# Two frequency-domain filters with a gate: a padded scratch and another order of its rows

## The chip, the core and the metric

The kernel runs on one core of a Trainium2 chip. A core has five engines with instruction streams of their own: TensorE (PE, with a separate stream of weight loads, PEld), VectorE (DVE), ScalarE (ACT), GpSimd (POOL) and SyncE (SP), which here only issues DMAs. The DMAs of a core are carried out by 16 DMA engines between the device memory (HBM) and the on-chip memory (SBUF, 128 partitions). The metric is the device time of one execution in microseconds.

## The reference

An input `x` of 2048 x 1024 goes through two filters, A and B: a real 2-D Fourier transform, a product with a complex weight (one per filter), and the inverse transform. A gate per row, from a dot product of the row with `gate_w`, mixes the two results.

```python
def _A_ref(x, w_r, w_i):                       # B alike
    X = rfft2(x.astype(float32), axes=(-2, -1))
    W = w_r + 1j * w_i
    X = X * W
    return irfft2(X, s=(S, D), axes=(-2, -1)).astype(bfloat16)

x = A_x
g = sigmoid((x * gate_w).sum(-1, keepdims=True))
out = g * _A_ref(x, A_w_r, A_w_i) + (1 - g) * _B_ref(x, B_w_r, B_w_i)
```

Both filters see the same `x`, so the forward transform is made once.

## The kernel before

All transforms are matrix products with constants. The 1024 columns are split into even and odd frequencies (`par` 0 and 1), and the 2048 rows are transformed in two steps (a transform over 64 and one over 32). The order of all work is written out by hand in the string `ORDER`, one token per step; a letter names the step, the numbers its unit, and the letters behind the colon the engines that move its results out of the accumulator (PSUM). A scheduler adds nothing: each engine runs its instructions in the order in which the tokens issue them.

- `r`, `f`, `E`, `O` (`f1`): first step of the forward transform, from `x` into `Y`.
- `F` and `G` (`f2`, `f3`): the transform along the columns and the second step along the rows, for 16 units `n` of 128 frequencies (`n` from 0 to 7 even, from 8 to 15 odd half).
- `w` (`load_w`, L229): the weights of a unit from HBM, most of them issued ahead of the string; `c` (`cmul`, L416) multiplies by them; `d` (`edge`) does the edge columns.
- `i` (`i1`, L454): first step of the inverse transform of a unit. Its constant is `WI`, made by `make_constants` on the host, whose columns set the order of the 128 rows that come out. When both of its halves are done, the result (`rl`, 128 partitions x 4 blocks x 1 KB) is stored in the scratch in HBM by one DMA on SP's queue (L462).
- `q` (`fetch`, L471): a DMA on SP's queue that reads rows of four units back from the scratch, onto 64 partitions (even or odd ones, by `g`) of 8 KB each. `q1.0.2` reads for the odd half, units 0 to 3 of it, quarter `v` = 2 of the rows. The scratch thus does a transposition: what was spread over partitions within one unit comes to lie along one partition. SP waits for the stores of these four units before it issues the first of their reads.
- `j` (`i2`, L484): second step of the inverse transform, with the gate in its constants (`EAB`). Its `v` runs from 0 to 7, and two of them share one quarter: `j1.0` and `j1.1` need `q1.0.0` and `q1.1.0`; `j1.2` and `j1.3` need `q1.0.1` and `q1.1.1`; `j1.4` and `j1.5` those of quarter 2, `j1.6` and `j1.7` those of quarter 3.
- `k`, `D` (`i3`, `i3d`), `s` (`fold`) and `t` (`last`): the inverse transform along the columns, the sums and differences, and the stores of the output (L568 to L583).

The scratch is one tensor per half, of 8 units x 4 blocks x 128 rows x 1 KB, so a block is 128 KB and a unit 512 KB. Row `p` of a block is partition `p` of `rl`; in the order made by `be` in `make_constants`, the row is (j, v, c, r) with j of 2, v of 4, c of 2 and r of 8, and the eight rows of an r are one piece of 8 KB:

```python
sc = [scratch.tile([NU, 4, P, 512], BF16, name=f"sc{par}") for par in range(2)]
nc.sync.dma_start(sc[par][u].rearrange("t p f -> p t f"), rl[:].rearrange("p t a r m -> p (t a) (r m)"))
src = sc[par][4 * g:4 * g + 4].rearrange("u t (j v c r) f -> (u t j) v c (r f)", j=2, v=4, c=2)
nc.sync.dma_start((XP, RP)[par][v][g::2, 0:4096], src[:, v])
```

A read of quarter `v` takes 64 pieces: from each of 16 blocks the pieces (j, c) of that `v`, in this order on consecutive partitions of the target. `row_of` puts the rows of the gate's constant in the same order.

SP's queue, in order, holds the loads of `x`, constants and weights up to 28 us, then from 30 us the 16 stores and 16 reads of the scratch among the last weight loads, a late constant (`l`, L253) at 76 us, the eight reads of the odd half from 78 us, and the output from 90 us.

Of the kernel before, what the change touches and what calls it, by code (L numbers as in the profile page):

```python
# [10 lines left out]
P = 128  # L11
# [3 lines left out]
NU = 8  # L15
N1 = 32
N2 = 64
BF16 = mybir.dt.bfloat16
# [38 lines left out]
def _bf16np(a):  # L57
    return np.ascontiguousarray(np.asarray(a, dtype=np.float32).astype(ml_dtypes.bfloat16))


def block_k2(b):
    return (0, 32) if b == 0 else (b, 64 - b)


def block_rows(b):
    return np.array([k2 + 64 * k1 for k2 in block_k2(b) for k1 in range(N1)])
# [7 lines left out]
def row_of(ab, t, j, c):  # L74

    return 2 * (16 * (t // 2 % 4) + 8 * (t % 2) + 4 * ab + 2 * j + c) + t // 8


def make_constants():
    c = {}  # L80
    s2 = np.arange(N2)
    F = np.zeros((N2, 32, 2))
    EZ = np.zeros((32, 2, N2))
    E = np.zeros((P, N2))
    for b in range(32):
        k2 = block_k2(b)[0]
        th = 2 * np.pi * s2 * k2 / 64
        if b == 0:
            comps = (np.ones(64), np.cos(np.pi * s2))
            F[:, 0, 0], F[:, 0, 1] = comps  # L90
            EZ[0, 0], EZ[0, 1] = comps
        else:
            comps = (np.cos(th), np.sin(th))
            F[:, b, 0], F[:, b, 1] = np.cos(th), -np.sin(th)
            EZ[b, 0], EZ[b, 1] = 2 * np.cos(th), -2 * np.sin(th)
        for ab in range(2):
            for cc in range(2):
                E[row_of(ab, b // 2, b % 2, cc)] = comps[cc]
    F = F.reshape(N2, 64)
    F1 = np.concatenate([F, -F, F], axis=1)  # L100
    c["F1"] = _bf16np(np.concatenate([F1, F1], axis=0))
    c["E"] = _bf16np(E)
    c["EZ"] = _bf16np(EZ.reshape(64, 64) / 64)
    d = np.arange(256) + 0.5
    i = np.arange(256)
    FD = np.zeros((2, 2, 256, 256))
    IG = np.zeros((2, 2, 256, 256))
    for par in range(2):
        m = 2 * i + par
        ph = 2 * np.pi * np.outer(d, m) / D  # L110
        FD[par, 0] = np.cos(ph)
        IG[par, 0] = 2 * np.cos(ph).T
        if par == 0:
            IG[0, 0, 0] = 1
        m = 2 * i + (2 if par == 0 else 1)
        ph = 2 * np.pi * np.outer(d, m) / D
        FD[par, 1] = -np.sin(ph)
        IG[par, 1] = 2 * np.sin(ph).T
        if par == 0:
            IG[0, 1, 255] /= 2  # L120
    IG /= S * D
    c["FD"] = _bf16np(FD.reshape(2, 2, 2, 128, 256).transpose(3, 0, 2, 1, 4).reshape(128, 2, 1024))
    IGS = np.stack([-IG[1, 1], IG[1, 1]], axis=1).reshape(2, 128, 2, 256)
    c["IGU"] = _bf16np(IGS.transpose(1, 0, 2, 3).reshape(128, 1024))
    c["IG"] = _bf16np(IG.reshape(2, 2, 2, 128, 256).transpose(3, 0, 1, 2, 4).reshape(128, 2048))
    s1 = np.arange(N1)
    WF = np.zeros((P, NT, 3, 64))
    WI = np.zeros((P, NT, 4, 64))
    for t in range(NT):
        for j in range(2):  # L130
            b = 2 * t + j
            k = block_rows(b)
            al = np.zeros((2, N1, 64), dtype=complex)
            for p in range(64):
                w = np.exp(-2j * np.pi * k[p] * s1 / S)
                if b == 0:
                    al[p // 32, :, p] = w
                else:
                    al[0, :, p] = w
                    al[1, :, p] = 1j * (1 if p < 32 else -1) * w  # L140
            be = al.conj()
            if b > 0:
                be[1] = -be[1]
            al = al.transpose(1, 0, 2).reshape(64, 64)
            be = be.reshape(64, 64).T
            be = be.reshape(64, 2, 4, 8).transpose(0, 2, 1, 3).reshape(64, 64)
            h = slice(64 * j, 64 * j + 64)
            WF[h, t, 0], WF[h, t, 1], WF[h, t, 2] = al.real, al.imag, -al.imag
            h = h if t % 2 == 0 else slice(64 - 64 * j, 128 - 64 * j)
            WI[h, t, 0], WI[h, t, 1], WI[h, t, 2], WI[h, t, 3] = be.real, be.imag, -be.imag, -be.real  # L150
    c["WF"] = _bf16np(WF)
    c["WI"] = _bf16np(WI)
    c["SG"] = np.where(np.arange(P) // 8 % 2 == 0, 1.0, -1.0).astype(np.float32).reshape(P, 1)
    return c
# [3 lines left out]
def gated_mix(ctx, tc, x_in, we_in, wo_in, first_in, out):  # L158
    nc = tc.nc
    cn = make_constants()  # L160
    dr = {n: nc.inline_tensor(a, name=f"cst_{n.lower()}").ap() for n, a in cn.items() if n not in ("F1", "SG")}
    w_in = (we_in, wo_in)
# [15 lines left out]
    def take(tag, *dims):  # L178

        t = slots[tag][int(next(order[tag]))][:, 0:int(np.prod(dims))]  # L180
        ax = "abcd"[:len(dims)]
        return t.rearrange(f"p ({' '.join(ax)}) -> p {' '.join(ax)}", **dict(zip(ax, dims)))

    def halves():
        return [bank(), bank()]
# [24 lines left out]
    Ec = const.tile([P, N2], BF16, name="ec")  # L210
    Ez = const.tile([64, N2], BF16, name="ez")
    scratch = ctx.enter_context(tc.tile_pool(name="scratch", bufs=1, space=bass.MemoryType.DRAM))
    sc = [scratch.tile([NU, 4, P, 512], BF16, name=f"sc{par}") for par in range(2)]
    Y = big.tile([P, 2, 2, 2, 16, 2, 32, 2], BF16, name="y")
    y = [Y[:, par] for par in range(2)]
    wod = [big.tile([P, 2048], BF16, name=f"wo{k}") for k in range(4)]
# [45 lines left out]
    def evac(eng, out, in_):  # L262
        if eng == "A":
            nc.scalar.copy(out=out, in_=in_)  # L264
        else:
            nc.vector.tensor_copy(out=out, in_=in_)  # L266
# [6 lines left out]
    def hp(j):  # L273
        return slice(64 * j, 64 * j + 64)
# [168 lines left out]
    def i1(n, r, eng="A"):  # L443
        par, u = n // NU, n % NU
        p = Ps[n]
        o = 1 if par == 0 and r == 1 else 0
        ps = halves()
        terms = (((0, 0, 0), (2, 0, 1), (3, 1, 1), (2, 1, 0)), ((1, 0, 0), (0, 0, 1), (2, 1, 1), (0, 1, 0)))[r]
        terms = [z for z in terms if z[1:] not in summed.get(n, ())]
        for k, (w, q, a) in enumerate(terms):  # L450
            for tt in range(2):
                for j in range(2):
                    hin = hp(j ^ tt)
                    nc.tensor.matmul(ps[tt][hp(j), :], lhsT=WI[hin, 2 * u + tt, w, :],  # L454
                                     rhs=p[hin, q, tt, a::2, o:o + 256], start=(k == 0), stop=(k == len(terms) - 1))
        if r == 0:
            RLs[n] = take("rl", 2, 2, 2, 256)
        rl = RLs[n]
        for tt in range(2):
            evac(eng[tt % len(eng)], rl[:, tt, :, r, :], ps[tt][:].rearrange("p (a m) -> p a m", a=2))  # L460
        if r == 1:
            nc.sync.dma_start(sc[par][u].rearrange("t p f -> p t f"), rl[:].rearrange("p t a r m -> p (t a) (r m)"))  # L462
            RLs.pop(n), Ps.pop(n)

    def rows(par, v):
# [1 line left out]

    def fetch(par, g, v):

        src = sc[par][4 * g:4 * g + 4].rearrange("u t (j v c r) f -> (u t j) v c (r f)", j=2, v=4, c=2)  # L470
        nc.sync.dma_start((XP, RP)[par][v][g::2, 0:4096], src[:, v])  # L471

    Vs, EVs = {}, {}
# [114 lines left out]
    def run(tok):  # L588
        op, a, e = tok[0], tok[1:].split(":")[0], tok.split(":")[1] if ":" in tok else ""
        n = [int(q) for q in a.split(".")] if a else []  # L590
        if op in "rfEO":
            f1(((n[0], 0), (n[0], 1)) if op in "rf" else ((n[0], "EO".index(op)), (n[0] + 1, "EO".index(op))), e)
        elif op in "VQ":
            xfold(n[0], op)
        elif op == "y":
            gate_weights()
        elif op == "h":
            gt["z"] = gate_hat()
        elif op == "l":
            late()  # L600
        else:
            dict(F=f2, G=f3, d=edge, c=cmul, i=i1, w=load_w, g=gate_z, q=fetch, j=i2, k=i3, D=i3d,
                 s=fold, a=part, t=last)[op](*n, *([e] if e else []))
# [61 lines left out]
```

## Time and profile before

| What | Value |
|---|---|
| Median of 3 runs | 108.09 us (108.0 to 108.25) |
| The profiled execution | 107.94 us |
| Its span, first to last instruction | 106.2 us |
| Mean granted TensorE clock | 0.995 |
| DMA: bytes moved, mean rate | 37.06 MB, 349 GB/s |
| HBM read / written | 24.23 MB / 12.58 MB |
| Packets under 8 KB / all | 15840 / 16881 |
| SP's queue: share of 16 DMA engines | 92.4% |
| Stores and reads of the scratch together, issue to landing | 3.7, 5.9, 8.5 us (least, median, most) |
| Reads alone | 4.2, 6.5, 8.2 us |

The profile is of one execution. Busy times are the sums of an engine's instructions; the rest of the span is idle time. A row such as "PE pt L484 <- DMA ro<-sc: 1.5, 2, 1.2" in the list of waits says who waited (engine, tile, line), for whom, and how long in total, how often and at most. `pt` are accumulator tiles, `xr` and `ro` the SBUF tiles that hold first `x` and weights and later the rows read from the scratch (`xr` for the even, `ro` for the odd half). The DMA share is the mean busy share of the 16 DMA engines; it can exceed 1 in a short stretch, because a packet is booked whole where it starts. GB/s is what they moved. `SPq` and `PEldq` are the sequencers of SP and of the weight loads.

### The profile page before, as it was taken

How to read it: one execution, taken by the hardware profiler on the slowest of the kernel's cores; microseconds unless marked ns; L12 is line 12 of the kernel's file. 1: busy time of each engine (PE TensorE's matmuls, PEld its weight loads, DVE VectorE, ACT ScalarE, POOL GpSimd, SP SyncE). 2: the span in 40 equal slices, each digit the busy share in tenths (PEclk: the TensorE clock that was granted, in tenths of full speed). 3: DMA queues.
4: the chain of work that ended last, by engine and by line, in shares of the span. 5: the costliest groups of instructions: out<-in, count | busy, mean ns of one | idle time of the engine just before them, and what ended most of it. 6: DMA issues, size and time to landing. Idle time of an engine off the chain costs nothing. (4 is left out here: it accounts for less than half of the span.)

```text
span 106.2 us, 3918 instructions
## 1 busy us (share of the span) xinstructions
PE 97.6 (92%) x1606; PEld 66.3 (62%) x1608; DVE 90.5 (85%) x141; ACT 93.9 (88%) x187; POOL 8.5 (8%) x14
## 2 busy tenths in 40 slices
PE   5989999989999999999999999999999698999740
PEld 2378989655655766555765567667899485754530
DVE  1459998298999997999999999999989959899970
ACT  5069989998999999999999999999999878999740
POOL 1000001018880001000000000000000000000000
PEclk9999999999999999999999999999999999999997
DMA  2999999999999999999999699979989989967994
GB/s 44 336 350 420 402 395 396 406 422 397 398 405 410 399 379 358 394 367 368 374 371 387 204 376 384 367 278 342 358 264 279 355 321 377 409 275 321 392 350 133
DMA packets 16881, 37.06 MB, mean 349 GB/s; under 512 B 1628, under 2 KB 10464, under 8 KB 15840
## 3 DMA queue, kind: packets, MB, share of 16 engines
q1 hardware_dynamic: 16272, 36.37, 92.4%
q10 hardware_dynamic: 560, 0.45, 1.5%
q8 instruction: 12, 0.20, 0.7%
q14 instruction: 5, 0.04, 0.1%
q0 software_dynamic: 32, 0.00, 0.0%
HBM read 24.23 MB, written 12.58 MB: 347 GB/s over the span
## 5 line engine op out<-in xcount | busy, mean ns | idle before, releaser
L454 PE MATMUL pt<-p,wi 64*64 64x512 bf16 x504 | 30.3, 377 | 0.1
L264 ACT CAST rl<-pt 128x512 bf16<-128x512 f32 x47 | 25.6, 707 | 0.1
L416 DVE TENSOR_TENSOR p<-X,ro 128x4096 bf16<-128x4096 bf16 x11 | 25.2, 2294 | 0.0
L264 ACT CAST T<-pt 128x512 bf16<-128x512 f32 (+1 forms) x40 | 21.7, 623 | 0.9 <-PE pt L533 0.5
L454 PEld LDWEIGHTS <-wi 64*64 64x64 bf16 x504 | 15.1, 106 | 10.7 <-issue 0.8
L264 ACT CAST V<-pt 128x512 bf16<-128x512 f32 x29 | 17.2, 743 | 1.3 <-PE pt L484 1.3
L264 ACT CAST X<-pt 128x512 bf16<-128x512 f32 x29 | 16.8, 671 | 0.0
L376 PE MATMUL pt<-fd,y 128*128 128x256 bf16 x128 | 15.9, 273 | 0.0
L264 ACT CAST y<-pt 128x512 bf16<-128x512 f32 x21 | 11.1, 631 | 4.5 <-PE pt L298 3.2
L376 PEld LDWEIGHTS <-y 128*128 128x128 bf16 x128 | 11.6, 98 | 4.2 <-issue 2.9
L266 DVE CAST rl<-pt 128x512 bf16<-128x512 f32 x17 | 11.3, 683 | 0.1
L499 PE MATMUL pt<-ig,V 128*128 128x256 bf16 x88 | 10.8, 273 | 0.0
L395 PE MATMUL pt<-T,wf 64*64 64x512 bf16 (+2 forms) x192 | 9.4, 307 | 0.0
L575 DVE TENSOR_TENSOR rl<-wo,T 128x1024 bf16<-128x1024 bf16 (+1 forms) x16 | 8.9, 620 | 0.6 <-ACT T L264 0.5
L264 ACT CAST p<-pt 128x512 bf16<-128x512 f32 x14 | 9.3, 818 | 0.0
L552 DVE TENSOR_TENSOR wo<-p,pt 128x512 bf16<-128x512 bf16 x14 | 8.8, 682 | 0.6 <-ACT p L264 0.5
L416 DVE TENSOR_TENSOR p<-X,wo 128x4096 bf16<-128x4096 bf16 x4 | 9.1, 2281 | 0.0
L499 PEld LDWEIGHTS <-V 128*128 128x128 bf16 x88 | 8.0, 98 | 1.5 <-issue 0.4
L370 POOL TENSOR_SCALAR ro<-ro 128x8 bf16<-128x8 bf16 x7 | 7.0, 1013 | 23.2 <-DMA ro<-in_we_dram 23.2
L307 PE MATMUL pt<-f,xr 64*128 64x256 bf16 x112 | 7.1, 270 | 0.5 <-DMA xr<-in_x_dram 0.5
L266 DVE CAST y<-pt 128x512 bf16<-128x512 f32 x11 | 7.2, 684 | 0.4 <-PE pt L310 0.4
L281 DVE TENSOR_TENSOR rl<-xr 128x512 bf16<-128x512 bf16 x7 | 3.0, 424 | 4.7 <-DMA xr<-in_x_dram 4.6
(58 smaller groups left out, 98.8 us busy)
## 6 DMA issues: line engine op xcount, KB each, us to landing
sc<-rl SPq DMA_DIRECT2D x16, 512.0 KB, 5.5
xr<-sc SPq DMA_DIRECT2D x8, 512.0 KB, 6.3
ro<-sc SPq DMA_DIRECT2D x8, 512.0 KB, 6.6
ro<-in_we_dram SPq DMA_DIRECT2D x7, 516.0 KB, 8.6
xr<-in_x_dram SPq DMA_DIRECT2D x6, 512.0 KB, 7.4
out_dram<-rl SPq DMA_DIRECT2D x6, 512.0 KB, 3.2
wo<-in_wo_dram SPq DMA_DIRECT2D x4, 512.0 KB, 7.7
ro<-in_wo_dram SPq DMA_DIRECT2D x4, 512.0 KB, 6.5
```

Source lines behind the costliest of these rows:

```text
L264: nc.scalar.copy(out=out, in_=in_)
L266: nc.vector.tensor_copy(out=out, in_=in_)
L281: e.tensor_tensor(f[:, 0, :], x[j][:, 0:512], x[j][:, 512:1024], ALU.add)
L307: nc.tensor.matmul(pv[h][:, :, c, :, :].rearrange("p a e k -> p e a k"), lhsT=xs(j0, h, q), rhs=fs(h, 0, *st), start=(q == 0), stop=(q == 3))
L370: nc.gpsimd.tensor_scalar(Ws[n][:, :, :, 257:258], Ws[n][:, :, :, 256:257], -1.0, None, ALU.mult)
L376: nc.tensor.matmul(ps[tt][:, e * 256:e * 256 + 256], lhsT=y[par][:, c, e, t].rearrange("p b s k -> p (b s k)"), rhs=FD[:, par, c, e, :], s ...
L395: nc.tensor.matmul(ps[tt][ho, dst:dst + ln], lhsT=WF[hp(j), 2 * u + tt, w, :], rhs=T[hp(j), tt, src:src + ln], start=(k == 0), stop=(k == 2))
L416: nc.vector.tensor_tensor(po, xo, wo, ALU.mult)
L454: nc.tensor.matmul(ps[tt][hp(j), :], lhsT=WI[hin, 2 * u + tt, w, :], rhs=p[hin, q, tt, a::2, o:o + 256], start=(k == 0), stop=(k == len(te ...
L499: nc.tensor.matmul(po, lhsT=V[:, s, 2 * r + c, :], rhs=IG[:, par, 2 * r + c, :], start=(c == 0), stop=(c == 1))
L552: (nc.vector if eng == "V" else nc.gpsimd).tensor_tensor(ev[:, :, r, :], c_, s_, op)
L575: nc.vector.tensor_tensor(o4[:, k, h] if not isinstance(od, list) else o4[:, k.start, h], x, y_, op)
```

## The change

Three things, in one:

- Each block of 128 rows in the scratch gets 32 more rows that nothing writes or reads. Blocks lie 160 KB apart instead of 128, a unit takes 640 KB instead of 512.
- `make_constants` no longer reorders the columns of `be`. A unit's rows then come out as (c, v, r) within j. Seen as one index c of 4 (j and the old c), the row of a block is (c, v, r).
- The read takes from each of the 16 blocks four pieces of 8 KB that are 32 KB apart. Before, they were at 0, 8, 64 and 72 KB of a block, plus 16 KB times `v`; after, at 0, 32, 64 and 96 KB, plus 8 KB times `v`. The order of the 64 pieces on the target's partitions is the same, and so are `row_of` and all that follows.

```diff
@@ make_constants
             al = al.transpose(1, 0, 2).reshape(64, 64)
             be = be.reshape(64, 64).T
-            be = be.reshape(64, 2, 4, 8).transpose(0, 2, 1, 3).reshape(64, 64)
             h = slice(64 * j, 64 * j + 64)
@@ gated_mix
-    sc = [scratch.tile([NU, 4, P, 512], BF16, name=f"sc{par}") for par in range(2)]
+    sc = [scratch.tile([NU, 4, P + 32, 512], BF16, name=f"sc{par}") for par in range(2)]
@@ i1
         if r == 1:
-            nc.sync.dma_start(sc[par][u].rearrange("t p f -> p t f"), rl[:].rearrange("p t a r m -> p (t a) (r m)"))
+            nc.sync.dma_start(sc[par][u, :, 0:P].rearrange("t p f -> p t f"), rl[:].rearrange("p t a r m -> p (t a) (r m)"))
@@ fetch
-        src = sc[par][4 * g:4 * g + 4].rearrange("u t (j v c r) f -> (u t j) v c (r f)", j=2, v=4, c=2)
+        src = sc[par][4 * g:4 * g + 4].rearrange("u t p f -> (u t) p f")[:, 0:P].rearrange("k (c v r) f -> k v c (r f)", c=4, v=4)
         nc.sync.dma_start((XP, RP)[par][v][g::2, 0:4096], src[:, v])
```

## The prediction

> **What bounds the kernel now.** I read the page first: the busy times, the slices, and how long a DMA takes to land. A read of the scratch is `ro<-sc` or `xr<-sc`, a store `sc<-rl`.
>
> ```profile
> span 106.2 us, 3918 instructions
> PE 97.6 (92%) x1606; PEld 66.3 (62%) x1608; DVE 90.5 (85%) x141; ACT 93.9 (88%) x187; POOL 8.5 (8%) x14
> ...
> sc<-rl SPq DMA_DIRECT2D x16, 512.0 KB, 5.5
> xr<-sc SPq DMA_DIRECT2D x8, 512.0 KB, 6.3
> ro<-sc SPq DMA_DIRECT2D x8, 512.0 KB, 6.6
> ```
>
> Three engines stand between 85 and 92% over the whole span, so a DMA matters only where they run dry. The list of waits names those places for the scratch:
>
> ```profile
> PE pt L484 <- DMA ro<-sc: 1.5, 2, 1.2
> ...
> PEld L484 <- DMA ro<-sc: 0.6, 1, 0.6
> ```
>
> No row names `xr<-sc`: the eight reads of the even half are in time. Of the odd half two are late, and the timeline says when:
>
> ```profile
> 78.13 7.70 SPq L471 DMA_DIRECT2D ro<-sc  x8
> ...
> 85.05 1.00 PEld L484 LDWEIGHTS <-ro 128*128 128x128 bf16 x32 [1.43 <-issue]
> 85.08 1.09 PE L484 MATMUL pt<-eab,ro 128*128 128x64 bf16 x32 [1.18 <-DMA ro<-sc]
> ...
> 88.48 0.99 PEld L484 LDWEIGHTS <-ro 128*128 128x128 bf16 x32 [0.64 <-DMA ro<-sc]
> 88.48 1.11 PE L484 MATMUL pt<-eab,ro 128*128 128x64 bf16 x32 [0.36 <-DMA ro<-sc]
> ```
>
> TensorE starts `j1.0` at 85.08 after 1.18 us of nothing (it waits for reads 1 and 2 of this half, q1.0.0 and q1.1.0) and `j1.2` at 88.48 after 0.36 us (reads 3 and 4). ScalarE and VectorE drain with it. Here the program is bound by scratch reads; after `j1.2` the three engines are the bound again, since reads 5 and 6 land just as `j1.4` loads its weights (issued at 83.89, landing 7.1 us later: 91.0; weights at 91.09).
>
> Third, how fast these reads run: stretches of 1 us with TensorE, weight load, VectorE, ScalarE, GpSimd, and last the clock, DMA share and GB/s.
>
> ```profile
> 81.00:82.00 1.00, 1.00 (x19) 0.91 (x16) 0.81 (x3) 1.00 (x4) 0.00 (x0) 1.00 0.86 254
> 82.00:83.00 1.00, 1.00 (x12) 0.90 (x10) 1.00 (x2) 1.00 (x4) 0.00 (x0) 1.00 0.78 197
> 83.00:84.00 1.00, 0.89 (x9) 0.56 (x6) 1.00 (x3) 1.00 (x4) 0.00 (x0) 1.00 0.94 385
> 84.00:85.00 1.00, 0.00 (x0) 0.00 (x0) 0.89 (x2) 0.60 (x2) 0.00 (x0) 1.00 1.06 410
> ...
> 87.00:88.00 1.00, 1.00 (x11) 0.76 (x8) 1.00 (x3) 1.00 (x4) 0.00 (x0) 1.00 0.98 352
> ...
> 90.00:91.00 1.00, 0.95 (x5) 0.49 (x5) 1.00 (x2) 1.00 (x4) 0.00 (x0) 1.00 1.03 434
> ```
>
> A read moves 64 pieces of 8 KB. Share x 16 engines, divided by the pieces moved (GB/s / 8.192 per us), is the time of one piece on one DMA engine: 1.03 x 16 / 53 = 0.311 us at 90 to 91, but 0.444 us at 81 to 82 and 0.519 us at 82 to 83, 0.365 us at 87 to 88. Same size, same row, same queue, up to 1.7 times as long. A packet is booked whole where it starts, so one row is rough; sums over several are better. From 81 to 90, where almost nothing but these reads is under way, the shares sum to 8.38 and the pieces to 365: 134.1 us of engine time against 365 x 0.311 = 113.6 us. The excess is 20.5 / 16 = 1.28 us: 0.57 us of it from 81 to 83, 0.11 us from 83 to 85, 0.45 us from 85 to 88, 0.15 us to 90. This excess is the only thing of the kernel that addresses alone can change, and it lies ahead of the two waits.
>
> **The change part by part.** *The constants.* The reordering of the 64 columns of `be` is host work; WI keeps its size, and the 504 matmuls of L454 stay 377 ns each. Nothing. The order of instructions on every engine is the same but for line numbers.
>
> *Bytes and counts.* 16 stores of 512 KB, 16 reads of 64 pieces of 8 KB, as before; the gap is never written or read. The source of a read goes from 32 x 2 pieces to 16 x 4. SP issues a read in 0.60 us (median of the `ro<-sc` issues, 0.51 to 1.52); the nearest other row, a store with eight times the pieces, takes 0.37 us, so I take nothing for the issue, bounded by some 0.2 us either way on the first two reads.
>
> *The stores.* Each partition's four 1 KB pieces go 160 KB apart instead of 128. From 75 to 78 stores are nearly alone: mean share 1.06 at 362 GB/s, or 1.06 x 16 / 353 = 0.048 us a piece; the fastest stretch of them (77 to 78) has 0.047. There is nothing to gain in their rate. But the last store gates read 2: SP waits 1.68 us for it, until 80.4. Were it 0.6 us earlier, the whole 1.18 us could go; this is the far end. I take zero.
>
> *The reads.* Before, the pieces of one read sit at multiples of 64 KB plus 0 and 8 KB: pairs of 16 KB, all at one place within 64 KB. After, they sit at (5k + c) x 32 KB, k the block (0 to 15) and c the piece (0 to 3): if each engine works at one k, the sixteen stand on sixteen different multiples of 32 KB within 512 KB, where before they stood on the same one within 128 KB. The trace shows no such address pattern. Bounds: excess gone altogether (all pieces at 0.311 us, as at 90 to 91 with the old layout): 1.28 to 0 us. Or all pieces as slow as at 81 to 82: 365 x 0.133 / 16 = 3.0 us. The excess is largest where all engines start together after a gap in the reads (81 to 83) and zero once they have been running unevenly for a while, which looks like sixteen streams in step meeting at one place; spreading them bears on just that. Between the two rows (0.311 late, 0.444 to 0.519 early) I take half of the excess away, 0.64 us.
>
> In time: read 2 lands 0.29 us earlier (half of 0.57), so `j1.0` starts at 84.79. Reads 3 and 4 landed at 88.5 (issued at 81.7, 6.8 us); they come half of 1.13 = 0.57 us earlier, at 87.9, and `j1.2` wants them at 88.12 - 0.29 = 87.83. So `j1.2` starts at 87.9, 0.57 us earlier. Reads 5 and 6 land at 91.0 - 0.64 = 90.36; `j1.4` wants them at 91.09 - 0.57 = 90.52. Every later step is engine work that shifts along. **Sum: -0.6 us**, from a span of 106.2 to 105.6. This profiled execution took 107.94 us, 1.74 outside the span; the median of the runs is 108.09, 0.15 above it. Forecast 107.5.
>
> The Trainium skill speaks against it. On its page "DMA: Bandwidth & Descriptors", section "Latency and other measured facts", copies with rows 512 KiB apart still run at 207 GB/s a direction beside 214 for the padded layout, and only pitches of 2 MiB and up lose much (164, then 103). By that rule 128 KB is harmless and the sum is 108.1. The trace agrees in part: the pieces at 90 to 91 have the same pitch and lose nothing; it disagrees in that the pieces at 82 to 83 lose 0.2 us each.
>
> **The rivals.** *Addresses have nothing to do with it.* The excess comes from starting on an idle queue and from reading behind a burst of stores. For it: it fades with time since the last store (80.4), and at 78 to 79, where the late constant in rows of 2 KB shares the engines with the tail of the stores, the rate falls to 182 GB/s with a share of 0.84. Against it: at 85 to 88, 5 us past any store, 0.45 us are still lost. Time: 108.1. The rule of the Trainium skill named above leads to the same time.
>
> *The reads get worse.* Before, two pieces are one run of 16 KB and four reads walk through one run of 64 KB; after, no two pieces of a read touch. If a visited stretch stays quick to read, half of the pieces lose that. For it: the quick pieces at 90 to 91 are the last of a run whose neighbours were read just before. Price: excess up by half, `j1.0` +0.29, read 4 +0.57, so `j1.2` starts 0.57 late: 108.7. Doubled: read 4 +1.13, read 6 +1.28 of which 0.15 more: 109.3. At 3.0 us of excess: 2.37 times 1.13 is 1.55 us late, 109.7. It decides from the first piece lost, since neither wait has slack.
>
> *The read isn't spread as before.* Sixteen outer rows in place of 32 might be dealt to the engines less evenly, or the issue takes longer. Against it: 16 rows suit 16 engines. Some 0.5 us on read 2: 108.6 or more.
>
> **How the numbers follow.** Forecast 0.46; addresses without effect 0.18; reads worse 0.30; spread or issue worse 0.06. About 0.2% (0.2 us) is what a measurement of this kernel tells from no change. Faster 0.46, same 0.18, slower 0.36. The fast end takes the excess away whole (-0.93: `j1.0` 0.57, then the 0.36 of `j1.2`) and the last store 0.6 us sooner: -1.5, 106.6; the slow end is the doubled excess, 109.3. The forecast's own range is 106.9 to 107.8.
>
> **What would show it.** In the profile after: the wait of L484 on `ro<-sc` falls from 1.5 us to about 0.9; GB/s just after the first odd reads start rise from 197 and 254 to 300 or more; `ro<-sc` lands in some 6.1 us instead of 6.6; stores stay at 5.5. The forecast is wrong if those stretches stay at 0.44 us a piece or more, if the loss sits in stores, or if new waits on `xr<-sc` appear before 80 us.

## The result, and the profile after

The change makes the kernel slower: 114.32 us median of 6 runs (112.81 to 115.38) against 108.09 us before, a ratio of 1.0487 with a 95% interval of 1.0426 to 1.0547. Executions of one kernel fall into fast and slow ones, some per cent apart: here and below a median counts all, a ratio only the fast ones, and the traces of nat_pad4, nat_pad16, nat_pad128, same_places_16x4 and whole_odd are of slow ones. The profiled execution took 112.81 us with a span of 111.0 us, 4.8 us more than before. The code is one line shorter, so L483 here is L484 of before (`i2`), L470 is the read of the scratch and L461 the store.

The page of the changed kernel first: busy times, then the DMA issues with their size and the time from issue to landing.

```profile
PE 98.0 (88%) x1608; PEld 65.3 (59%) x1608; DVE 90.7 (82%) x141; ACT 94.4 (85%) x187; POOL 8.5 (8%) x14
...
sc<-rl SPq DMA_DIRECT2D x16, 512.0 KB, 5.6
xr<-sc SPq DMA_DIRECT2D x8, 512.0 KB, 8.7
ro<-sc SPq DMA_DIRECT2D x8, 512.0 KB, 8.5
```

The engines do almost the same work as before (98.0 us against 97.6 on TensorE, 94.4 against 93.9 on ScalarE). The median store lands as fast (5.6 against 5.5 us), reads of the scratch take some 2 us longer (8.7 and 8.5 against 6.3 and 6.6). The list of waits of the changed kernel shows who paid:

```profile
PE pt L483 <- DMA ro<-sc: 4.4, 4, 2.2
...
DVE rl L265 <- DMA sc<-rl: 2.2, 2, 1.7
...
ACT rl L263 <- DMA sc<-rl: 1.2, 2, 0.6
...
PE pt L483 <- DMA xr<-sc: 0.7, 1, 0.7
```

The last three are new. The even half's reads are now late too (`xr<-sc`), and VectorE and ScalarE wait for stores to leave the `rl` buffers. The median hides these stores: the three issued from 61 us land in 7.1 to 7.8 us where they took 5.6 to 6.7, and the last five, issued from 70 us on, in 4.5 to 5.7 where they took 3.7 to 4.6. That they lie behind the slow reads on the same queue is the likely reason; no view shows it directly. The timeline of the changed kernel gives the places:

```profile
65.20 0.64 PE L483 MATMUL pt<-eab,xr 128*128 128x64 bf16 x16 [0.70 <-DMA xr<-sc]
68.31 0.69 DVE L265 CAST rl<-pt 128x512 bf16<-128x512 f32 x1 [1.66 <-DMA sc<-rl]
...
87.81 1.09 PE L483 MATMUL pt<-eab,ro 128*128 128x64 bf16 x32 [2.23 <-DMA ro<-sc]
...
91.71 1.11 PE L483 MATMUL pt<-eab,ro 128*128 128x64 bf16 x32 [0.86 <-DMA ro<-sc]
...
95.85 0.63 PE L483 MATMUL pt<-eab,ro 128*128 128x64 bf16 x16 [1.15 <-DMA ro<-sc]
```

Against the same steps before, the delay grows in this way:

| Step | Before, us | After, us | Later by |
|---|---|---|---|
| `j0.0` starts | 64.32 | 65.20 | 0.9 |
| last store of the scratch issued | 75.8 | 77.7 | 1.9 |
| `j1.0` | 85.08 | 87.81 | 2.7 |
| `j1.2` | 88.48 | 91.71 | 3.2 |
| `j1.4` | 91.31 | 95.85 | 4.5 |
| `j1.6` | 94.84 | 99.71 | 4.9 |
| `j1.7` | 98.76 | 103.63 | 4.9 |

So 1.9 us come from the even half and the stores behind it, 3.0 us from the odd half's reads, and nothing behind them. How fast these reads run is seen in the stretch from 86 to 93 us (columns: TensorE, weight load, VectorE, ScalarE, GpSimd, granted clock, DMA share, GB/s), first before, then after:

```profile
86.00:93.00 7.00, 6.58 (x98) 4.83 (x96) 6.59 (x13) 6.61 (x15) 0.00 (x0) 1.00 0.95 375
```

```profile
86.00:93.00 7.00, 4.33 (x81) 3.50 (x82) 4.67 (x10) 4.11 (x9) 0.00 (x0) 1.00 1.02 262
```

All 16 DMA engines are busy and move only 262 GB/s. By the arithmetic of the prediction (share x 16, divided by pieces of 8 KB per us) one piece keeps an engine 1.02 x 16 / 32.0 = 0.51 us, where it was 0.95 x 16 / 45.8 = 0.33 us. It stays at 262 in nearly every microsecond of this stretch: a ceiling, not a loss at the start.

### The profile page after: what moved, and what is told of

It reads as the page before. It is cut to its first block, busy times and chain, and to the rows that moved or that the text cites. A ratio compares the mean times of both kernels' runs of the same rounds, so it can differ in the third digit from the quotient of the medians.

```text
span 111.0 us, 3920 instructions
## 1 busy us (share of the span) xinstructions
PE 98.0 (88%) x1608; PEld 65.3 (59%) x1608; DVE 90.7 (82%) x141; ACT 94.4 (85%) x187; POOL 8.5 (8%) x14
## 5 line engine op out<-in xcount | busy, mean ns | idle before, releaser
L263 ACT CAST V<-pt 128x512 bf16<-128x512 f32 x29 | 16.0, 644 | 4.0 <-PE pt L483 3.9
L483 PE MATMUL pt<-eab,ro 128*128 128x64 bf16 x128 | 4.7, 193 | 4.4 <-DMA ro<-sc 4.4
L263 ACT CAST p<-pt 128x512 bf16<-128x512 f32 x14 | 8.3, 700 | 0.0
L483 PEld LDWEIGHTS <-ro 128*128 128x128 bf16 x128 | 4.3, 98 | 6.1 <-issue 4.7
```

The source lines that it names most:

```text
L483: nc.tensor.matmul(ps[s][:, ch * 128 + h * 64:ch * 128 + h * 64 + 64], lhsT=R[:, k, ch * 128:ch * 128 + 128], rhs=EAB[:, 4 * v + k, :], st ...
```

## The experiments

Three things changed at once: the order of the rows, the gap, and with them the way in which a read's source is told to the DMA. Each kernel below is the changed one with an edit; "a piece" is the time of one 8 KB piece on one DMA engine, worked out as above from a stretch of the odd half's reads. The fences show the main lines of each edit; the others are left out.

### Order alone, and smaller gaps

```diff
-    sc = [scratch.tile([NU, 4, P + 32, 512], BF16, name=f"sc{par}") for par in range(2)]
+    sc = [scratch.tile([NU, 4, P, 512], BF16, name=f"sc{par}") for par in range(2)]   # nat_pad0; P + 4, P + 8, P + 16 in the others
```

> Natural order alone, blocks 128 KB apart, nothing unused. Theory PLACE (a read is slow when all of its 8 KB pieces stand on the same place within 32 KB): pieces still stand on one place, so as slow as the change: 112 to 115 us, 0.45 to 0.52 us of a DMA engine per 8 KB piece in the odd half's reads. Theory GAP (the 160 KB distance of the blocks does the harm): back to 107.5 to 108.5 us and 0.31 to 0.37 us a piece. Theory RUN (what is lost is that two pieces were one run of 16 KB): 112 to 115 us.

> Natural order, 4 KB unused behind each block: eight places 4 KB apart within 32 KB. PLACE: 106.5 to 108.5 us, 0.31 to 0.36 us a piece. GAP: 108 to 112 us, a small gap harms less. RUN: 112 to 115 us.

> Natural order, 8 KB unused behind each block, so that the blocks of one read stand on four places within 32 KB. PLACE: 106.5 to 108.5 us, 0.31 to 0.36 us a piece. GAP: a gap harms, 110 to 115 us. RUN: still no two pieces touch, 112 to 115 us, 0.45 to 0.52 us a piece.

> Natural order, 16 KB unused behind each block: two places within 32 KB. PLACE: between the others, 107 to 110 us, 0.33 to 0.42 us a piece. GAP: 110 to 115 us. RUN: 112 to 115 us, 0.45 to 0.52 us a piece.

Without a gap the natural order is as fast as the kernel before: 107.86 us median against 107.89, ratio 0.9982 (0.994 to 1.0024). Each gap, of 4, 8 or 16 KB, is as bad as 32: ratios 1.051 (1.0392 to 1.0628), 1.0597 (1.0484 to 1.071) and 1.0515 (1.0388 to 1.0642), with 0.53, 0.55 and 0.57 us a piece (90 to 97 us). That a small gap harms less, 108 to 112 us at 4 KB, was expected under GAP and is not so: the median there is 113.69 us. nat_pad0 from 87 to 91 us, then nat_pad8 from 90 to 97:

```profile
87.00:91.00 4.00, 2.98 (x45) 2.04 (x44) 3.96 (x10) 3.04 (x7) 0.00 (x0) 1.00 1.01 422
```

```profile
90.00:97.00 7.00, 5.67 (x63) 3.64 (x62) 5.65 (x12) 4.88 (x9) 0.00 (x0) 0.82 1.02 241
```

nat_pad0 needs 1.01 x 16 / 51.5 = 0.31 us a piece with no two pieces touching and all of them at one place within 32 KB: RUN and PLACE fall. Of what was written down only GAP is left. But a gap does two things: it moves addresses, and it keeps the source from being joined. Without it, 16 blocks of 4 pieces lie 32 KB apart throughout and are told as 64 pieces at one distance; with it, as 16 x 4. The kernel before was told as 32 x 2. This is read off the code; no view shows the list that reaches the DMA engines.

### The same places told in another way, and gaps told in another way

```diff
# same_places_16x4: no gap; the four pieces of a block from last to first, and the gate's rows with them
-    return 2 * (16 * (t // 2 % 4) + 8 * (t % 2) + 4 * ab + 2 * j + c) + t // 8
+    return 2 * (16 * (t // 2 % 4) + 8 * (t % 2) + 4 * ab + 3 - 2 * j - c) + t // 8
+        t = sc[par][4 * g:4 * g + 4]
+        src = bass.AP(t.tensor, t.offset + 49152 + 4096 * v, [[65536, 16], [-16384, 4], [1, 4096]])
# nat_pad128: P + 128 rows a block
# half_pad16: 16 rows unused behind every 64 (half_pad0: none), a store in two halves, 32 x 2 with the gap
+    sc = [scratch.tile([NU, 4, 2, 64 + 16, 512], BF16, name=f"sc{par}") for par in range(2)]
+            for j in range(2):
+                nc.sync.dma_start(sc[par][u, :, j, 0:64].rearrange("t p f -> p t f"), rl[hp(j)].rearrange("p t a r m -> p (t a) (r m)"))
+        src = sc[par][4 * g:4 * g + 4].rearrange("u t j p f -> (u t j) p f")[:, 0:64].rearrange("k (c v r) f -> k v c (r f)", c=2, v=4)
```

> No gap, blocks 128 KB apart, natural order, every piece where nat_pad0 has it; only the list of a read's source is told as 16 blocks of 4 pieces, the four taken from last to first (the gate's rows follow), so that it can't be joined into 64 pieces at one distance. Theory DEAL (what costs is that the source is told as 16 x 4 and not 32 x 2 or 64, so that the pieces are dealt to the DMA engines in another way): 112 to 115 us, 0.48 to 0.57 us of a DMA engine per 8 KB piece in the odd half's reads. Theory ADDRESS (the distances of 132 to 160 KB in memory cost): as nat_pad0, 107.5 to 108.5 us, 0.31 to 0.38 us a piece.

> A gap of 128 KB: blocks 256 KB apart, a power of two, source 16 x 4. DEAL: 112 to 115 us, 0.48 to 0.57 us a piece. ADDRESS: as nat_pad0, 107.5 to 108.5 us, 0.31 to 0.38 us a piece.

> 16 KB unused behind each half block of 64 rows, so blocks are 160 KB apart as in the change, but a read's source is 32 half blocks of 2 pieces. Each store is two DMAs of 64 partitions. DEAL: 0.31 to 0.38 us a piece in the odd half's reads, and about the time of half_pad0 (108 to 110 us, the halved stores are new). ADDRESS: 0.48 to 0.57 us a piece, 112 to 116 us.

> Natural order, no gap, each store as two DMAs of 64 partitions: the control for half_pad16. Both theories: 0.31 to 0.38 us a piece, 107.5 to 110 us; what it loses to nat_pad0 is the price of the halved stores.

same_places_16x4 reads the very bytes that nat_pad0 reads, and takes 114.93 us (ratio 1.052, 1.04 to 1.064). Its reads from 91 to 99 us:

```profile
91.00:99.00 8.00, 7.07 (x82) 4.92 (x81) 6.69 (x13) 6.10 (x13) 0.00 (x0) 0.80 1.03 258
```

That is 0.52 us a piece. The low TensorE clock in this row (0.80) is not the reason: the change has 0.51 us at 1.00, and whole_odd, below, 0.32 at 0.50. Nor is it that the four pieces of a block are taken backwards, since the kernels with a gap take them forwards and are as slow. half_pad16 has blocks 160 KB apart like the change, told as 32 x 2; from 91 to 95 us:

```profile
91.00:95.00 4.00, 3.53 (x49) 2.55 (x50) 3.97 (x10) 3.58 (x8) 0.00 (x0) 1.00 1.00 412
```

That is 0.32 us a piece. nat_pad128, blocks 256 KB apart and 16 x 4, is slow (0.54 us, ratio 1.0455, 1.0366 to 1.0543). The piece times of each of the three alone go against ADDRESS, and DEAL's hold in all: **what costs is that the source is told as 16 x 4**, not where the bytes lie. The two kernels with halved stores are slow for another reason, 32 stores in place of 16: half_pad0 needs 0.32 us a piece as well (94 to 100 us) and takes 116.67 us (ratio 1.0733, 1.0605 to 1.0861), where both theories expected 107.5 to 110; half_pad16 takes 115.15 us (1.0436, 1.0332 to 1.054), outside the 108 to 110 us of DEAL. By its time alone half_pad16 would fit ADDRESS (112 to 116); its 0.32 us a piece, and its control half_pad0, which is slow without any gap, decide against that. In half_pad0's profiled execution TensorE's clock fell to 0.50 from 92 to 96 us; why the one with the gap is the faster of these two stays open.

### Reads alone: what is wrong with 16 x 4

A kernel of reads alone, six of each kind, one kind after the other; each group waits for the one before. The names of the forms are left out here.

```python
FORMS = [([[16384, 64]], 2), ([[32768, 32], [4096, 2]], 2), ([[65536, 16], [8192, 4]], 2),  # source, step of target partitions
         ([[65536, 16], [8192, 4]], 1), ([[16384, 64]], 1), ([[32768, 32], [4096, 4]], 1), ([[65536, 16], [4096, 8]], 1)]
src = bass.AP(x.tensor, x.offset + 4096 * (k % 2), [list(z) for z in form] + [[1, 4096]])
nc.sync.dma_start(T[k][0:n * step:step, :] if step > 1 else T[k][0:n, :], src)
```

> All of the computation is left out: seven groups of six reads of the input, one group after the other, all in pieces of 8 KB to partitions of 8 KB, that differ in how the source is told and in the target's partitions. Target every second of 128 partitions: (1) 64 pieces at one distance, (2) 32 x 2, (3) 16 x 4. Target 64 neighbouring partitions: (4) 16 x 4, (5) 64 at one distance. Target all 128: (6) 32 x 4, (7) 16 x 8. Theory PORT (partitions come in fours that share a way into the on-chip memory; a DMA engine is given whole outer rows of the source; a row that covers two fours makes two engines meet on each way, and 64 neighbouring partitions have only half of the ways): 0.31 us of an engine per piece in (1), (2), (6); 0.45 to 0.6 in (3) and (7); 0.58 to 0.62 in (4) and (5). Theory OUTER16 (a source of 16 outer rows is dealt worse whatever the target): 0.31 in (1), (2), (5), (6); 0.45 to 0.6 in (3), (4) and (7). Theory STEP (pieces at an uneven distance are slow to read in memory): 0.31 in (1) and (5), slower in all others.

Stretches inside groups 2 to 7, in this order (columns: VectorE, GpSimd, clock, DMA share, GB/s):

```profile
21.00:30.00 9.00, 0.00 (x0) 0.00 (x0) 1.00 0.90 340
35.00:47.00 12.00, 0.00 (x0) 0.00 (x0) 1.00 0.99 234
52.00:66.00 14.00, 0.00 (x0) 0.00 (x0) 1.00 0.99 205
71.00:85.00 14.00, 0.00 (x0) 0.00 (x0) 1.00 0.99 207
90.00:104.00 14.00, 0.00 (x0) 0.00 (x0) 1.00 1.01 420
110.00:135.00 25.00, 0.00 (x0) 0.00 (x0) 1.00 1.02 230
```

| Group | Target partitions | Source | us a piece |
|---|---|---|---|
| 2 | 64, every second | 32 x 2 | 0.35 |
| 3 | 64, every second | 16 x 4 | 0.55 |
| 4 | 64 neighbours | 16 x 4 | 0.63 |
| 5 | 64 neighbours | 64 | 0.63 |
| 6 | all 128 | 32 x 4 | 0.32 |
| 7 | all 128 | 16 x 8 | 0.58 |

(Group 1, 64 pieces at one distance to every second partition, was paced by VectorE clearing its tiles at the start and gives no steady rate. From 14 to 17.5 us, at a share of 0.71 and 257 GB/s, it needs 0.36 us a piece, so it is nearer to groups 2 and 6 than to the rest.) OUTER16 and STEP both expected group 5 fast; with group 4 it is the slowest, though its source is the plainest of all: the target alone does that. And group 6 is fast with four pieces to an outer row, which rules out the count of four. PORT has the order of all six right, with groups 2, 4 and 5 a little above its numbers (0.31, and 0.58 to 0.62): apart from the 64 neighbours, an outer row is fast when its pieces go to one group of four partitions (two pieces on every second partition, or four on neighbours) and slow when they go to two groups (four on every second, eight on neighbours).

A plainer rule fits as well, and no run here parts the two. Apart from the 64 neighbours, every list with 16 outer rows is slow and every list with 32 or more is fast, in this table and in all the filter kernels. Group 4 has 16 rows that each stay within one group of four, but there group 5, with 64 rows, is just as slow.

On the ports, the Trainium skill has this on its page "SBUF — State Buffer", section "Door 1: The DMA port swizzle": the partitions come in aligned fours, each four belongs to one of 16 ports, partitions 0 to 63 reach only 8 of these, and a transfer to 64 neighbouring partitions measured 196 GB/s, with 218 as its limit. Groups 4 and 5 agree with their 205 and 207 GB/s. That a DMA engine is given whole outer rows, so that with 16 x 4 two engines meet on a port, is an inference that the table allows and does not prove; no view here tells which engine moved which piece. Nor do the runs explain why the slow reads of the filter kernels vary between 0.51 and 0.57 us a piece.

### The gap with aligned fours, and an attempt to win

```diff
# all128_pad32 (all128_pad0: P in place of P + 32): one read of a quarter for both g
-    return 2 * (16 * (t // 2 % 4) + 8 * (t % 2) + 4 * ab + 2 * j + c) + t // 8
+    return 16 * (t // 2 % 4) + 8 * (t % 2) + 4 * ab + 2 * j + c + 64 * (t // 8)
-    c["SG"] = np.where(np.arange(P) // 8 % 2 == 0, 1.0, -1.0).astype(np.float32).reshape(P, 1)
+    c["SG"] = np.where(np.arange(P) // 4 % 2 == 0, 1.0, -1.0).astype(np.float32).reshape(P, 1)
+        if g == 0:
+            return
+        src = sc[par].rearrange("u t p f -> (u t) p f")[:, 0:P].rearrange("k (c v r) f -> k v c (r f)", c=4, v=4)
+        nc.sync.dma_start((XP, RP)[par][v][:, 0:4096], src[:, v])
# whole_odd: no gap, rows as before; only the odd half in reads of 1 MB
+                src = sc[1].rearrange("(g u) t (c v r) f -> (u t c) g v (r f)", g=2, c=4, v=4)
+                nc.sync.dma_start(RP[v][:, 0:4096], src[:, :, v])
```

> The change's scratch with its gap of 32 KB, natural order, one store a unit; but the two reads of a quarter are one of 1 MB, 32 blocks of 4 pieces onto all 128 partitions, a block's four pieces on four neighbouring partitions that share a way. PORT: 0.31 to 0.36 us of an engine per piece in the odd half although the source has the same gap and is told as 32 x 4; 107.5 to 110 us (the first reads start later, since they wait for all eight units). ADDRESS: 0.48 us or more a piece and 113 us or more.

> As all128_pad32 without the gap, so the source is 128 pieces at one distance. PORT: 0.31 to 0.36 us a piece and the same time as all128_pad32 within 1%. ADDRESS: 107.5 to 110 us, 3% or more faster than all128_pad32.

> Natural order, no gap. Even half read as in nat_pad0; in the odd half the two reads of a quarter are one of 1 MB, told as 64 x 2 so that an outer row covers two neighbouring partitions of one way. PORT: 0.31 to 0.36 us a piece; the first quarter can't start before the last store has landed, but the reads behind it run without a break: 107 to 109 us. OUTER rows that are short cost by themselves: 0.4 us a piece or more, over 110 us.

With fours that are aligned, and 32 outer rows in place of 16, the same gap of 32 KB costs nothing. all128_pad32 and all128_pad0 have ratios of 1.0247 (1.016 to 1.0335) and 1.0248 (1.0168 to 1.0328), and their reads from 86 to 91 us, with the gap and without:

```profile
86.00:91.00 5.00, 3.50 (x55) 2.79 (x53) 3.42 (x6) 3.68 (x9) 0.00 (x0) 1.00 1.01 428
```

```profile
86.00:91.00 5.00, 3.34 (x53) 2.66 (x51) 3.27 (x6) 3.52 (x8) 0.00 (x0) 1.00 1.02 431
```

Both 0.31 us a piece. The first 3 us of their odd half's reads, again with the gap and without:

```profile
84.30:87.30 3.00, 2.58 (x24) 2.06 (x22) 3.00 (x6) 3.00 (x7) 0.00 (x0) 1.00 0.94 322
```

```profile
83.80:86.80 3.00, 2.90 (x34) 2.38 (x30) 2.87 (x5) 3.00 (x8) 0.00 (x0) 1.00 0.97 339
```

The 2.5% that both lose to the kernel before go with reads of 1 MB, which wait for all eight units; no run takes that apart further. Their medians, 110.83 and 110.73 us, are within 1% of each other, as PORT had it, and just above the 107.5 to 110 that it expected with the gap. whole_odd is fast in its reads too, 0.32 us a piece:

```profile
88.00:92.00 4.00, 4.00 (x44) 3.30 (x42) 2.55 (x5) 2.80 (x5) 0.00 (x0) 0.50 1.00 408
```

It loses 2% (1.0196, 1.0113 to 1.028), with 110.17 us above the 107 to 109 expected: TensorE waits 3.4 us for the first quarter, which can't start before the last store has landed. No version here beats the kernel before; nat_pad0 equals it.

## Why the prediction was wrong

- **Bytes and counts.** The prediction named the step, "the source of a read goes from 32 x 2 pieces to 16 x 4", and costed it at nothing but for the issue. This is the step that failed: it took a transfer to be its pieces, and put the way in which they are told at nothing. same_places_16x4 shows the price of that alone: 0.52 us a piece where nat_pad0 has 0.31, and 5.2% of the time before. The rival that had it, "the read isn't spread as before", was given a chance of 0.06 and 0.5 us on one read. "16 rows suit 16 engines", the only reason given against it, did not hold: all 16 are busy (share 1.02), and yet each piece takes longer. What makes it longer inside the transfer (two engines on one port, or 16 rows as such) stays open.
- **The reads.** The forecast's own mechanism, streams in step at one place that the gap would spread, isn't there. In the two kernels with reads of 1 MB, the first 3 us of the odd half's reads lose the same with the gap as without: 0.94 x 16 / 39.3 = 0.38 us a piece in all128_pad32 (84.3 to 87.3 us) and 0.97 x 16 / 41.4 = 0.37 in all128_pad0 (83.8 to 86.8). So the excess at the start is not the gap's to mend. Nor was it what the prediction read from its averages, 0.2 us lost on each piece at 82 to 83 us: by the single packets in the trace of before, 28 of the 53 pieces that start between 81 and 83 us take 0.31 to 0.32 us, and 12 take 0.70 to 1.13. In the changed kernel all 224 pieces between 86 and 93 us take 0.41 to 0.60. The old loss sits in a few pieces, the new one in every piece; what makes the few slow stays open.
- **Addresses without effect.** The rival was right about addresses, and so was the rule of the Trainium skill beside it (page "DMA: Bandwidth & Descriptors", section "Latency and other measured facts"): with blocks 128 KB apart (nat_pad0) and 160 KB apart (all128_pad32) the reads run at 0.31 us a piece. Its time of 108.1 us was wrong all the same, since the gap acts by another way than addresses.
- **The reads get worse.** Right in sign, wrong in cause: losing runs of 16 KB costs nothing (nat_pad0). Its sums stopped at 3.0 us of lost engine time (109.7 us, although the slow end was named as 109.3); from 86 to 93 us alone the loss is now 224 pieces x 0.2 / 16 = 2.8 us.
- **Where the delay lands.** That "after `j1.2` the three engines are the bound again" no longer holds: reads 5 and 6 come late as well, and `j1.4` waits 1.15 us. That the even half had slack (no row named `xr<-sc`) was right, but how much was not asked; 2 us more per read used it up, and with the stores that came late behind the reads it cost 1.9 us before the odd half's reads could all begin. The prediction named "new waits on `xr<-sc` appear before 80 us" as a sign of its failure, and they are there.
- **The stores and the constants.** The constants cost nothing, as predicted, and the median store landed as predicted (5.6 us against 5.5). But "I take zero" for the stores left out that they come behind reads, which are now slower: of the last eight, six took 0.7 to 1.8 us longer from issue to landing, and engines waited for them.

## What to carry to other kernels

A gap in a DRAM layout also changes how the DMA is told: dims that were joined come apart. In these runs a read ran at full rate when its source had 32 or more outer rows, the pieces of each row went to one aligned group of four partitions, and the target spanned all 128 partitions; which of the first two conditions counts is not settled, so keep both. To tell a layout's effect from that of its telling, read the same bytes with another list. If GB/s sits at one low number while the DMA share is 1, look at the list and the target before you blame the addresses.

## What the hardware showed that was not expected

- Reads of the same bytes to the same 64 partitions run at 422 GB/s or at 258, by the way the source is told.
- 64 neighbouring partitions take 205 to 207 GB/s, half of the 420 that all 128 take.
- Distances of 32 KB, 160 KB or pairs of 16 KB make no difference that these runs can tell: 0.31 to 0.33 us a piece in all of them.
